# Seven-product gate projection in two more token groups, q weighted by another engine, stores on another queue

## The chip, the cores, the metric

One core of one Trainium2 chip. The metric is the device time of one execution in microseconds (us), median of several runs. Every run used below is in the fast state; a difference of half a per cent matters here, so most kernels were timed in five rounds beside the kernel before, on the same chip.

## The reference

q, k, v are 8 x 8 x 576 x 64 (batches, heads, positions, head size).

```python
r = np.maximum(x, 0.0); phi = np.concatenate([r * cos_w, r * sin_w], axis=-1)   # for q and k
kv  = np.einsum('bhsf,bhsd->bhfd', k_p, v);  z = np.sum(k_p, axis=2)
x   = np.einsum('bhsf,bhfd->bhsd', q_p, kv) / (np.einsum('bhsf,bhf->bhs', q_p, z) + 1e-06)
g   = x @ w_gate                     # x as 4608 tokens x 512, w_gate and w_val 512 x 1536
out = (silu(g) * (x @ w_val)) @ w_out
```

## The kernel before

It works through nine groups of 512 tokens (0 to 8). A group has a **gate and value stage** (gate = x W_gate, silu, times x W_val) and an **output stage** (times W_out). Beside these, TensorE makes the x tiles of the next group (four of 128 tokens each) and, once per batch, the product kv. The other work of attention is laid into numbered slots: a group has 16, twelve in the gate and value stage and four in the output.

TensorE's products land in banks of PSUM, and in this program a product waits until the bank that it writes has been read. In the groups of `GATE` the gate is made block-wise with seven products in place of eight (sums and differences of blocks first, then fewer products). Everything on an engine runs in the order in which it was issued, and that order is what the change works on:

```python
GATE = (7, 8)
...
for u in range(3):                       # ffn_by_quarters: a third of the gate each
    product(a, u, A11, B11, True)
    nc.scalar.copy(out=b, in_=a)         # PSUM to PSUM
    product(e, u, W3, X3, True)          # W: differences of weights, X: differences of x
    nc.scalar.copy(out=m7, in_=e)
    V(...)                               # one row of the value projection
    done()                               # the slot: an x tile, kv, a step of q, k or v
    product(b, u, W2, X2, False)
    nc.vector.tensor_tensor(out=c, in0=m7, in1=b, op=ALU.add)      # "the c add"
    product(a, u, A12, B21, False)
    silu(u, 1, 0, a)                     # ScalarE
    if u:
        mul(u - 1, 1, 1)                 # VectorE: silu times value, gives ht
    V(...); done()
    product(b, u, W1, X1, False)
    nc.vector.tensor_tensor(out=m7, in0=m7, in1=b, op=ALU.add)
    ...                                  # two more products, silus, values, muls
    if u == 2:
        for n in (1, 2):
            token_sum(n, 0, 4)           # VectorE: sums of ht for the output's seven products
    mul(u, 0, 0)
    mul(u, 1, 0)
    ...
def load_behind(b):                      # loads of batch b, once the turn of batch b-1 has landed
    nc.gpsimd.tensor_copy(out=hold2, in_=phit[b - 1][0:1, :, 0, 0, 0])
    load(b, "q")
    if b > 3:
        load_kv(b)
```

An x tile is a TensorE product and three VectorE operations (sum, reciprocal, multiply: 1.06 us), then a transposing DMA (its "turn"). A q batch is relu on ScalarE, a cosine and sine weighting on VectorE (0.75 us for each of four head pairs), then two transposing DMAs. kv leaves PSUM by two copies on ScalarE and, after them, two on VectorE.

Of the kernel before, what the change touches and what calls it, by code (L numbers as in the profile page):

```python
# [18 lines left out]
def kernel(  # L19
# [10 lines left out]
    nc = tc.nc  # L30
# [20 lines left out]
    KH = KC // 2  # L51
    GATE = (7, 8)

# [223 lines left out]
    def phi_q(b, g):  # L277

        if g == 0:
# [4 lines left out]
                                in1=tab, op=ALU.mult)  # L284

    def vmul(b, g):
        nc.vector.tensor_tensor(  # L287
            out=v2s[b == 1][:, g, :, :, 0:D],
            in0=(first if b == 0 and g == 0 else {"v": raw_of(b, "v")})["v"][:, g].unsqueeze(2).to_broadcast([P, NC, 2, D]),
            in1=tab, op=ALU.mult,  # L290
        )
# [144 lines left out]

    def a_tile2(t):

        (b0, c0), (b1, c1) = (divmod(2 * t + r, NC) for r in range(2))
        ps = take(2)  # L440
        if b0 == b1:
            parts = [(slice(0, P), b0, c0, 2)]
        else:
            parts = [(slice(0, SH), b0, c0, 1), (slice(SH, P), b1, c1, 1)]
        for e in range(2):
            for g in range(G):
                for ms, b, c, n in parts:
                    nc.tensor.matmul(  # L448
                        out=ps[ms, e, g * D1:(g + 1) * D1],
                        lhsT=phit[b][:, e, g, c:c + n].rearrange("p c s -> p (c s)"),  # L450
                        rhs=kv2s[b % 2][:, e, g // 2, g % 2], start=True, stop=True,
                    )
        x_of(t, ps)

# [152 lines left out]
    def ffn_by_quarters(tg, slot_of):  # L607
# [37 lines left out]
        for u in range(3):  # L645
# [12 lines left out]
            c = bank("c", seeded=True)  # L658
            nc.vector.tensor_tensor(out=c, in0=m7, in1=b, op=ALU.add)
            product(a, u, A12, B21, False)  # L660
            silu(u, 1, 0, a)
            free("a")
            if u:
                mul(u - 1, 1, 1)
            V(u, 0, 0) if u else V(u, 1, 0)
            done()
            product(b, u, W1, X1, False)
            nc.vector.tensor_tensor(out=m7, in0=m7, in1=b, op=ALU.add)
            silu(u, 0, 1, m7)
            product(c, u, A22, X4, False)  # L670
            silu(u, 0, 0, c)
# [16 lines left out]
            if u:  # L688
                done()
                token_sum(*((3, 0, 4) if u == 1 else (4, 0, 4)))  # L690
        V(2, 1, 1)
# [29 lines left out]

    def ffn_out(t, f0=0, f1=None):

        f1 = FC if f1 is None else f1
        if f0 == 0:
            o_ps[t] = take(1, ("o", t), fills=True)
        r = t % OUT * P
        for fc in range(f0, f1):
            nc.tensor.matmul(out=o_ps[t], lhsT=ht[:, fc, r:r + P], rhs=wo_sb[:, fc],  # L729
                             start=(fc == 0), stop=(fc == FC - 1))  # L730
        if f1 < FC:
            return
        ps = o_ps.pop(t)
        give_back(("o", t))
        if t % 2 == 0:
            nc.scalar.mul(out=ob_of(t), in_=ps, mul=DOWN)
        else:
            nc.vector.tensor_single_scalar(out=ob_of(t), in_=ps, scalar=DOWN, op=ALU.mult)
        store(t)

# [26 lines left out]
    def out_by_quarters(tg, slot_of):  # L767

        last = tg == NTG - 1
        t0 = tg * OUT  # L770
        for t in (t0, t0 + 2):
# [43 lines left out]
        for p_, o_, x_ in each(b, c[0], C22):  # L815
            nc.vector.scalar_tensor_tensor(out=o_, in0=x_, scalar=UP, in1=p_, op0=ALU.mult, op1=ALU.add)
        token_sum(4, 4, 6)
        slot_of(0)
# [14 lines left out]
        if last:  # L833
            store_two(t0 + 2, slice(0, HD))
        else:
            for t in (t0 + 2, t0 + 3):
                store(t)
        slot_of(2)
# [3 lines left out]
        for t in (t0, t0 + 1):  # L842
            store(t, *((slice(HD, d_model), (nc.sync, nc.scalar)) if last else ()))
        slot_of(3)
# [151 lines left out]
    def load_behind(b):  # L996

        nc.gpsimd.tensor_copy(out=hold2, in_=phit[b - 1][0:1, :, 0, 0, 0])  # L998
        load(b, "q")
        if b > 3:  # L1000
            load_kv(b)

    def load_kv(b):
# [14 lines left out]
    for b in range(2, B):  # L1018
        s0 = SLOTS * (b - 1)
        keng = "dve" if b == 2 else "act"  # L1020
        steps = [lambda b=b, g=g: phi_q(b, g) for g in range(G)]
        steps += [lambda b=b, g=g: (relu_k(b, g, g + 1, keng), vmul(b, g)) for g in range(G)]
        if b == 2:
            fs, tq = [s0 + i for i in (0, 0, 1, 1, 4, 5, 5, 6)], (s0 + 2, s0 + 2)
        else:
# [4 lines left out]
            at(p0 + 3 if b < 5 else p0 + 1, lambda b=b: load_behind(b))  # L1030
        tk = (s0 + 4, s0 + {2: 8, 3: 7}.get(b, 5))
        for s, f in zip(fs, steps):
# [5 lines left out]
    for t in range(2 * OUT, NTG * OUT):  # L1038
        tg, i = divmod(t, OUT)
        s = SLOTS * (tg - 1) + (5 if tg > 2 else 4) + 2 * i  # L1040
        if t == 2 * OUT:
            at(s, a_(t, 0))
            at(s + 1, a_(t, 1), turn(t))
        elif tg == 2:
            at((9, 10, 11)[i - 1] + SLOTS, lambda t=t: a_tile2(t), turn(t))
            if i == 2:
                at(11 + SLOTS, load_3)
        else:
            if t in (13, 14, 15):
                s = SLOTS * 2 + t - 4  # L1050
            elif tg - 1 in GATE:
                s = SLOTS * (tg - 1) + ((1, 2, 7, 9) if tg < 6 else (1, 2, 4, 7) if tg < 8 else (1, 2, 5, 6))[i]
            at(s, lambda t=t: a_tile2(t), turn(t))
    for tg in range(1, NTG):
# [12 lines left out]
        for i in range(OUT):  # L1067
            ffn_out(tg * OUT + i)
            weight_sum(i)
# [32 lines left out]
```

## Time and profile before

| what | value |
|---|---|
| time | 316.44 us (316.44 to 316.55, 3 runs) |
| span of the profiled execution | 314.5 us, clock 1.00 |
| TensorE | 98% busy, 2696 matmuls |

The page gives busy time by engine, the stretches view the same between two times, and the timeline lists single operations: start, length, engine, source line, operation, output and input by name, and in brackets how long the engine sat idle before it and what released it. The prediction below shows the main lines. One more place is needed for the comparison, the output stage of group 4, from the timeline of the kernel before:

```profile
175.80 1.47 PE L786 MATMUL banks<-wo_sb,ht 128*128 128x256 f16 x12
177.10 2.78 PE L786 MATMUL banks<-wt_sb,sums 128*128 128x256 f16 x24
179.11 1.25 ACT L266 ACTIVATE raw_q<-raw_q 128x576 bf16<-128x576 bf16 x2
179.72 1.47 PE L786 MATMUL banks<-wo_sb,ht 128*128 128x256 f16 x12
```

TensorE runs its first 48 output products without a bracket, that is without waiting. Later in this stage it pauses for 0.21 us before the last twelve products and for 0.12 us after them, by the starts of its rows against its pace. ScalarE's relus of the next q stand behind the silus of the group, in the output stage.

### The profile page before, as it was taken

The numbers are of one execution on the slowest core, as the hardware profiler recorded it, in microseconds if no ns is written. First come the engines' busy times: TensorE is split into PE (matmuls) and PEld (weight loads), VectorE is DVE, ScalarE is ACT, GpSimd is POOL, SyncE is SP. The second block draws the span as 40 slices with busy tenths as digits, with TensorE's granted clock in tenths as the row PEclk, the third lists the DMA queues.
The fourth block names the chain that finished last, engine by engine and source line by source line (L and its number), as shares of the span: only waits on it lengthen the run. The fifth ranks groups of instructions, "written<-read, shape, count | busy, mean of one in ns | idle before, by whom it ended". The sixth has DMA issues, their size and how long they took to land.

```text
span 314.5 us, 6775 instructions
## 1 busy us (share of the span) xinstructions
PE 307.5 (98%) x2696; PEld 189.7 (60%) x2696; DVE 228.2 (73%) x458; ACT 143.4 (46%) x264; POOL 36.0 (11%) x62
## 2 busy tenths in 40 slices
PE   8899999999999999999999999999999999999994
PEld 4597455455444585548654764577456866687673
DVE  7873777697678888587748786778779478946772
ACT  7554545763335346334543454335533345324530
POOL 7855102000200200030003000300000000000000
PEclk9999999999999999999999999999999999999999
DMA  7999999996897994989495979598951160014004
GB/s 268 217 198 197 206 205 138 226 133 99 143 208 114 150 145 110 148 119 196 100 153 75 200 144 154 73 192 135 164 86 35 40 145 17 20 38 98 0 2 133
DMA packets 74767, 41.07 MB, mean 131 GB/s; under 512 B 49904, under 2 KB 69872, under 8 KB 74736
## 3 DMA queue, kind: packets, MB, share of 16 engines
q1 hardware_dynamic: 51952, 22.55, 38.0%
q0 software_dynamic: 22192, 17.57, 37.2%
q10 hardware_dynamic: 592, 0.52, 0.5%
q8 instruction: 21, 0.34, 0.4%
q14 instruction: 10, 0.08, 0.1%
HBM read 37.75 MB, written 9.44 MB: 150 GB/s over the span
## 4 chain that ended last, share of the span: by engine, by line
PE 91%; DVE 5%; ACT 2%; issue 1%; ACTq 0%
PE banks L564 46%; PE banks L786 20%; PE banks L729 6%; PE banks L633 5%; PE banks L621 5%; PE banks L333 3%; PE banks L448 3%; DVE ht L638 1%; PE banks L494 1%; PE banks L430 1%; DVE v L287 1%; DVE sums L760 1%; DVE x L471 1%; PE banks L197 1%; PE banks L536 0%
## 5 line engine op out<-in xcount | busy, mean ns | idle before, releaser
L564 PE MATMUL banks<-xT,wg_sb 128*128 128x512 f16 (+2 forms) x368 | 86.6, 360 | 0.0
L564 PE MATMUL banks<-xT,wv_sb 128*128 128x512 f16 (+2 forms) x368 | 86.6, 360 | 0.0
L570 ACT ACTIVATE sg<-banks 128x512 bf16<-128x512 f32 (+2 forms) x92 | 51.5, 560 | 76.0 <-PE banks L564 74.0
L575 DVE TENSOR_TENSOR ht<-sg,banks 128x512 f16<-128x512 bf16 (+2 forms) x92 | 57.9, 637 | 29.7 <-PE banks L564 22.7
L564 PEld LDWEIGHTS <-wv_sb 128*128 128x128 f16 x368 | 35.5, 98 | 37.4
L564 PEld LDWEIGHTS <-wg_sb 128*128 128x128 f16 x368 | 33.9, 98 | 31.5 <-issue 0.2
L786 PEld LDWEIGHTS <-ht 128*128 128x128 f16 x336 | 32.5, 98 | 4.2
L786 PEld LDWEIGHTS <-sums 128*128 128x128 f16 x252 | 24.5, 98 | 4.2 <-issue 0.8
L633 PE MATMUL banks<-xT,wv_sb 128*128 128x512 f16 x96 | 24.3, 379 | 0.0
L283 DVE TENSOR_TENSOR r_q<-raw_q,tab 128x1152 bf16<-128x1152 bf16 x24 | 17.6, 754 | 7.4 <-ACT raw_q L266 7.1
L729 PE MATMUL banks<-wo_sb,ht 128*128 128x512 f16 x96 | 22.7, 379 | 0.0
L471 DVE TENSOR_TENSOR x<-banks,rec 128x512 f16<-128x512 f32 (+1 forms) x32 | 21.6, 674 | 1.3 <-PE banks L430 0.3
L786 PE MATMUL banks<-wo_sb,ht 128*128 128x256 f16 x168 | 20.6, 273 | 0.0
L287 DVE TENSOR_TENSOR v<-raw_v,tab 128x1152 bf16<-128x1152 bf16 x27 | 19.9, 751 | 0.5 <-ACT raw_v L849 0.5
L786 PE MATMUL banks<-wt_sb,sums 128*128 128x256 f16 x168 | 19.8, 273 | 0.1
L786 PE MATMUL banks<-wt_sb,ht 128*128 128x256 f16 x168 | 19.5, 273 | 0.0
L799 ACT ACTIVATE ob<-banks 128x512 f32<-128x512 f32 x14 | 8.4, 597 | 21.9 <-PE banks L786 21.9
L638 DVE TENSOR_TENSOR ht<-sg,banks 128x512 f16<-128x512 bf16 x24 | 15.5, 681 | 2.4 <-ACT sg L627 2.4
L266 ACT ACTIVATE raw_k<-raw_k 128x576 bf16<-128x576 bf16 (+1 forms) x25 | 17.1, 694 | 0.0
L998 POOL COPY hold<-phit 1x2 bf16<-1x2 bf16 x5 | 1.4, 287 | 129.3 <-DMA phit<-r_q 129.3
L760 DVE TENSOR_TENSOR sums<-ht 128x1024 f16<-128x1024 f16 (+1 forms) x28 | 15.5, 553 | 0.4
L266 ACT ACTIVATE raw_q<-raw_q 128x576 bf16<-128x576 bf16 x24 | 15.4, 675 | 0.0
(121 smaller groups left out, 334.6 us busy)
## 6 DMA issues: line engine op xcount, KB each, us to landing
out_dram<-ob SPq DMA_DIRECT2D x67, 128.0 KB, 2.5
raw_k<-in_k_dram POOLq DMA_DIRECT2D x7, 576.0 KB, 8.8
raw_q<-in_q_dram POOLq DMA_DIRECT2D x6, 576.0 KB, 6.0
raw_v<-in_v_dram POOLq DMA_DIRECT2D x6, 576.0 KB, 11.4
wo_sb<-in_moe_w_out_dram POOLq DMA_DIRECT2D x3, 512.0 KB, 12.8
wg_sb<-in_moe_w_gate_dram POOLq DMA_DIRECT2D x5, 256.0 KB, 9.4
wv_sb<-in_moe_w_val_dram POOLq DMA_DIRECT2D x5, 256.0 KB, 9.5
wo_sb<-in_v_dram SPq DMA_DIRECT2D x2, 576.0 KB, 4.0
```

The lines of the kernel that those rows point to most:

```text
L266: nc.scalar.activation(out=out, in_=in_, func=AF.Relu)
L283: nc.vector.tensor_tensor(out=st[b, "q"][:, g], in0=o.unsqueeze(2).to_broadcast([P, NC, 2, D]), in1=tab, op=ALU.mult)
L287: nc.vector.tensor_tensor(out=v2s[b == 1][:, g, :, :, 0:D], in0=(first if b == 0 and g == 0 else {"v": raw_of(b, "v")})["v"][:, g].unsquee ...
L471: nc.vector.tensor_tensor(out=st["x", t].rearrange("p (y e d) -> p e y d", e=2, d=D)[:, :, ys], in0=ps[:, :, 0:2 * J * D1].rearrange("p e ...
L564: nc.tensor.matmul(out=st["f", tg, fc, lo][i], lhsT=(wg_sb, wv_sb)[i][:, kc, fs], rhs=xT[tg][:, ts, kc], start=(kc == 0), stop=(kc == KC - 1))
L570: nc.scalar.activation(out=sg[:, 0:n], in_=st["f", tg, fc, lo][0], func=AF.Silu, scale=DOWN)
L575: nc.vector.tensor_tensor(out=ht[:, fc, r:r + n], in0=st.pop(("s", tg, fc, lo))[:, 0:n], in1=ps[1], op=ALU.mult)
L633: nc.tensor.matmul(out=val[u, i, w], lhsT=wv_sb[:, kc, fc * P:(fc + 1) * P], rhs=xT[tg][:, :, kc], start=(kc == 0), stop=(kc == KC - 1))
L638: nc.vector.tensor_tensor(out=ht[:, fc], in0=gates[u, w][:, i], in1=val.pop((u, i, w)), op=ALU.mult)
L729: nc.tensor.matmul(out=o_ps[t], lhsT=ht[:, fc, r:r + P], rhs=wo_sb[:, fc], start=(fc == 0), stop=(fc == FC - 1))
L760: nc.vector.tensor_tensor(out=o[:, lo:hi], in0=x[:, lo:hi], in1=y[:, lo:hi], op=op)
L786: nc.tensor.matmul(out=to[i][:, 0] if len(to) == 2 else to[0][:, i], lhsT=a[:, kc, i * P:(i + 1) * P], rhs=b[:, kc], start=first and kc == ...
```

## The change

The intent: save TensorE time in each of groups 5 and 6 (the prediction works out 1.21 us), and take work and waits out of VectorE's way there, so that the saving arrives.

```diff
-    GATE = (7, 8)
+    PHI_ACT = 7
+    GATE = (5, 6, 7, 8)
+    def phi_q_part(b, c, w):                       # q of batch 7: relu(cos * q) in one ScalarE pass
+        nc.scalar.activation(out=st[b, "q"][:, :, c, w], in_=raws[b, "q"][:, :, c], func=AF.Relu,
+                             scale=csk[:, c, w:w + 1])
 ... a_tile2 (an x tile)
-        x_of(t, ps)
+        if later:
+            behind.append(lambda: (x_of(t, ps), give_back(("a2", t)), x_turn(t)))
+        else:
+            x_of(t, ps)
 ... ffn_by_quarters
             nc.vector.tensor_tensor(out=c, in0=m7, in1=b, op=ALU.add)
+            while behind:
+                behind.pop(0)()
-            if u:
-                mul(u - 1, 1, 1)
 ...
             silu(u, 0, 1, m7)
+            if u:
+                mul(u - 1, 1, 1)
 ...
-                token_sum(*((3, 0, 4) if u == 1 else (4, 0, 4)))
+            if u == 1:
+                token_sum(3, 0, 4)
 ... out_by_quarters, groups 1 to 7
+        queues = (nc.gpsimd, nc.gpsimd) if tg > 0 else None
-        token_sum(4, 4, 6)
+        token_sum(4, 0 if tg in GATE else 4, 6)
-                store(t)
+                store(t, queues=queues)
 ... load_behind: q of batch 7 is loaded with batch 6
+        if PHI_ACT <= b + 1 < B:
+            load(b + 1, "q")
 ... slots of q, k, v (p0: first slot of the group before), kv, and x tiles
+            if b >= PHI_ACT:
+                for i in range(2 * NC):
+                    at(p0 + 4 + i // 2, lambda b=b, i=i: phi_q_part(b, *divmod(i, 2)))
+                fs, tq = [p0 + 12, p0 + 13, p0 + 14, p0 + 15], (p0 + 13, p0 + 13)
+            elif b > 3:
+                f0 = p0 + {4: 12, 5: 10}.get(b, 8)
+                fs, tq = [f0 + i for i in (...)], ...
-        tk = (s0 + 4, s0 + {2: 8, 3: 7}.get(b, 5))
+        tk = (s0 + 4, s0 + (3 if b - 1 in GATE else {2: 8, 3: 7}.get(b, 5)))
-                s = SLOTS * (tg - 1) + ((1, 2, 7, 9) if tg < 6 else (1, 2, 4, 7) if tg < 8 else (1, 2, 5, 6))[i]
+                s = SLOTS * (tg - 1) + ((0, 3, 7, 9) if tg < 6 else (0, 2, 5, 7) if tg < 8 else (0, 3, 5, 7))[i]
+                if s % SLOTS in (0, 3, 7):
+                    at(s, lambda t=t: a_tile2(t, True))
+                    continue
+            elif tg in GATE:                       # x tiles made in group 4: slots 5, 7, 9, 11 before
+                s = SLOTS * (tg - 1) + (2, 4, 7, 9)[i]
 ... (some small lines left out)
```

More of the change, by code (lines that the diff above doesn't have):

```diff
@@ L284, in phi_q @@
                                 in1=tab, op=ALU.mult)
+    def phi_q_part(b, c, w):
+        if (b, "q") not in st:
+            st[b, "q"] = rel.tile([P, G, NC, 2, D], BF16, name="r_q")
+        nc.scalar.activation(out=st[b, "q"][:, :, c, w], in_=raws[b, "q"][:, :, c], func=AF.Relu,
+                             scale=csk[:, c, w:w + 1])
     def vmul(b, g):
@@ L435, in a_tile, with a_tile2 @@
                 )
-    def a_tile2(t):
+    behind = []
+    def a_tile2(t, later=False):
         (b0, c0), (b1, c1) = (divmod(2 * t + r, NC) for r in range(2))
-        ps = take(2)
+        ps = take(2, ("a2", t) if later else None)
         if b0 == b1:
@@ L720, in store_two, with ffn_out @@
                 in_=obs[t // 2][e * SH:(e + 1) * SH, :, cols])
-    def ffn_out(t, f0=0, f1=None):
+    def ffn_out(t, f0=0, f1=None, queues=None):
         f1 = FC if f1 is None else f1
@@ L836, in out_by_quarters @@
             for t in (t0 + 2, t0 + 3):
-                store(t)
+                store(t, queues=queues)
         slot_of(2)
@@ L842, in out_by_quarters @@
         for t in (t0, t0 + 1):
-            store(t, *((slice(HD, d_model), (nc.sync, nc.scalar)) if last else ()))
+            store(t, *((slice(HD, d_model), (nc.sync, nc.scalar)) if last else (slice(0, d_model), queues)))
         slot_of(3)
@@ L998, in load_behind @@
         nc.gpsimd.tensor_copy(out=hold2, in_=phit[b - 1][0:1, :, 0, 0, 0])
-        load(b, "q")
+        if b < PHI_ACT:
+            load(b, "q")
         if b > 3:
             load_kv(b)
+        if PHI_ACT <= b + 1 < B:
+            load(b + 1, "q")
     def load_kv(b):
@@ L1020 @@
         keng = "dve" if b == 2 else "act"
-        steps = [lambda b=b, g=g: phi_q(b, g) for g in range(G)]
+        steps = [lambda b=b, g=g: phi_q(b, g) for g in range(G)] if b < PHI_ACT else []
         steps += [lambda b=b, g=g: (relu_k(b, g, g + 1, keng), vmul(b, g)) for g in range(G)]
@@ L1030 @@
             at(p0 + 3 if b < 5 else p0 + 1, lambda b=b: load_behind(b))
-        tk = (s0 + 4, s0 + {2: 8, 3: 7}.get(b, 5))
+            if b >= PHI_ACT:
[4 more added lines that the diff above has]
+                f0 = p0 + {4: 12, 5: 10}.get(b, 8)
+                fs, tq = [f0 + i for i in ((0, 0, 1, 2, 3, 4, 5, 6) if b == 4 else range(8))], (f0 + (3 if b == 4 else 4),) * 2
+        tk = (s0 + 4, s0 + (3 if b - 1 in GATE else {2: 8, 3: 7}.get(b, 5)))
         for s, f in zip(fs, steps):
@@ L1067 @@
         for i in range(OUT):
-            ffn_out(tg * OUT + i)
+            ffn_out(tg * OUT + i, queues=(nc.gpsimd, nc.gpsimd))
             weight_sum(i)
```

## The prediction

> **What bounds the kernel now.** I read the page of the profile first: its list of engines and the chain that ended last.
>
> ```profile
> PE 307.5 (98%) x2696; PEld 189.7 (60%) x2696; DVE 228.2 (73%) x458; ACT 143.4 (46%) x264; POOL 36.0 (11%) x62
> ```
>
> TensorE is busy all through, and the chain is 91% TensorE. So a change pays by what it takes off TensorE's stream of matmuls, and costs by every gap it puts into it. Next I cut the trace at the starts of the token groups (512 tokens each), by the stretches view; columns are the stretch, its length, then PE, PEld, DVE, ACT, POOL busy, clock, DMA share, GB/s. The rows are groups 4, 5, 6, 7; 7 (and 8) already form the gate projection from seven block products.
>
> ```profile
> 152.70:185.32 32.62, 32.59 (x294) 19.46 (x292) 24.14 (x46) 14.85 (x27) 2.40 (x4) 1.00 0.83 140
> 185.32:217.83 32.51, 32.48 (x285) 19.70 (x286) 24.74 (x47) 14.85 (x27) 2.91 (x4) 1.00 0.87 141
> 217.83:250.26 32.43, 32.43 (x295) 19.69 (x293) 23.13 (x45) 12.27 (x22) 0.00 (x0) 1.00 0.49 86
> 250.26:281.13 30.87, 30.37 (x251) 22.07 (x249) 22.95 (x45) 12.26 (x22) 0.00 (x0) 1.00 0.24 52
> ```
>
> Group 7 has 1.6 us less than group 6, but 1.18 of that is a kv product it has not got. The chain in order of time (start, length, what) gives TensorE's pace: 16 matmuls of 512 columns in 3.45 us, 215.6 ns each; 8 of 256 in 0.87, 108.8 ns each.
>
> ```profile
> 130.67 1.18 PE banks L333 x71
> 132.21 3.45 PE banks L564 x16
> 250.26 0.87 PE banks L621 x8
> 251.13 0.86 PE banks L633 x4
> ```
>
> At this pace group 7 needs 84 x 0.1088 (gate) + 48 x 0.2156 (value) + 4 x 0.26 (attention tiles) + 9.33 (output, as in other groups) = 29.9 us. It took 30.87: 1.0 us of gaps. TensorE's and then VectorE's rows of the timeline show two of them (start, length, ..., idle before).
>
> ```profile
> 256.26 0.60 PE L621 MATMUL banks<-xT,wg_sb 128*128 128x256 f16 x4
> 257.20 0.60 PE L621 MATMUL banks<-kvt,wgs_sb 128*128 128x256 f16 x4 [0.35 <-DVE x L471]
> ```
>
> ```profile
> 274.36 0.43 DVE L760 TENSOR_TENSOR sums<-ht 128x512 f16<-128x512 f16 x1
> ```
>
> The matmuls of 256.26 were issued by 256.70; the next waited until 257.20, 0.5 us, for the bank that the x step was reading. The token sum of 274.36 ends at 274.79, and the output product that reads it goes on at 274.84, 0.6 us late. A seven-product group lives at VectorE's limit.
>
> **What the Trainium skill says.** "TensorE: Matmul & The Clock Gate", section "Back-to-back issue gap", gives N/2.4 + 2.5 ns: 216 for 512 columns, 109 for 256. The trace agrees (215.6, 108.8); the page's "sustained" 131 ns for 512 it does not show. "PSUM — Partial Sum Buffer", section "PSUM bank collisions raise a hardware error", wants accesses of ScalarE and VectorE to one bank guarded; so VectorE's kv copies wait for ScalarE's, in the list of waits 6.6 us over 6. "Trainium Kernel Development and Optimization", section "Key Constraints", says that issuing from another engine saves issue time alone, as all queues share the DMA engines. In the trace a GpSimd issue occupies it 0.75 us. "ScalarE: Activation LUTs", section "What it computes", has func(scale * in + bias): relu and cosine weight in one pass.
>
> **The change part by part.** *Seven products in groups 5 and 6.* Out: 48 x 0.2156 = 10.35 us. In: 84 x 0.1088 = 9.14. Saved 1.21 us a group on the path, 2.4 in all: 0.8% of 316.4. This is the ceiling of the intent. It adds per group: 6 adds of 0.6 us on VectorE (start to start in a row), 4 input sums of 0.43, and 6 ScalarE copies of 0.58.
>
> *The last q by ScalarE.* 8 operations less on VectorE and ScalarE (4 x 0.754, 4 x 0.675), 18 of 256 columns in. ScalarE's relu takes 675 ns for 576 columns and 1156 for 1152, so 0.19 + 0.00084 per column: 0.41 us each, an estimate, 7.3 us in group 5. ScalarE has room (about 12 busy before), but in order: two of these in front of a silu delay its multiply by up to 0.8.
>
> *Stores on GpSimd's queue.* 56 issues x 0.75 = some 42 us of an engine at 11%. The transposes on the sync queue no longer queue behind eight stores (about 5.8 us). TensorE waits for no transpose now, so this itself gives nothing; it allows the earlier slots.
>
> *Group 4.* The order of instructions shows q's weighting moved from the output slots into slots 8 to 11, three of the four (0.72 each) ahead of the last token sum. Before, that sum ended 1.5 us after the output stage began (177.42 against 175.96), with VectorE almost without idle from 168.8. It will end at about 1.5 + 2.2 = 3.7; the product reading it needs it 2 x 1.31 + 0.44 = 3.06 after the start. **Loss 0.6.**
>
> *Group 5, by walking its order with these durations.* Its first product with a difference of x waits for the weight sum (0.95): 0.1. After slot 2 the same bank as in group 7 waits for x: 0.5. Then the kv product: after it ScalarE copies (0.76), VectorE copies (0.87), then c's add (0.69), with latencies 2.5 us, as the three muls leave no more work ahead; TensorE has only two products and a value row, 0.44 + 0.44 + 0.86 = 1.74. Loss 0.75, in group 5 the value row's bank even waits for the silu: 0.85. At the output some 0.15. Total 1.6 against 1.21 saved: **+0.4**. *Group 6:* the same without the weight sum, 1.3: **+0.1**.
>
> *Group 7.* The first x is put behind c's add, the second goes to slot 3, and one token sum (0.6) moves into the output stage. Left is about 0.45 for a bank at slot 3 and 0.1 at the output, of 1.0: **-0.4**. Groups 0 to 3 and 8: nothing.
>
> Sum: 0.6 + 0.4 + 0.1 - 0.4 = +0.7, so 317.1 from the walk. The gaps overlap less well on paper than on a chip (where one engine is late, the next wait shrinks), and the change is plainly laid out to avoid them; without any gap it would be 316.44 - 2.4 - 0.9 = 313.1. I choose 316.2, some three quarters of the way from 313.1 to 317.1.
>
> **Rivals.** (1) *The gaps are filled.* For it: deferred x steps, a mul moved behind an add, and group 8, already of this kind, whose gate and value stage ran without gaps. Against: groups 5 and 6 also have kv, x and, in 5, v's weighting. It would make 313 to 314.5. (2) *VectorE becomes the bound.* In group 5 it has some 22.7 us of work before the output against TensorE's 21.7; if it idles where it waits for kv, the stage becomes 24 and the time 317.5 to 318. (3) *GpSimd gets late.* Loads stand behind eight stores in its order (6 us), and the next q, k, v come later: in groups 3 to 5 ScalarE would wait for them. Against: loads are issued a third of a group ahead of use, and take 6 to 11 us. A miss would cost 1 to 3 us. (4) *ScalarE's 18 small passes* delay silus: up to 0.8 more in group 5.
>
> **Range and chances.** The walk and the gapless case differ by 4 us; I take 314.4 to 317.8, most of it. 2% is 6.3 us: a gain of that size exceeds the ceiling, and a loss needs two rivals at once. Faster 0.02, within 0.96, slower 0.02. Which side of 316.44 is nearly a coin toss, with a little more on faster.
>
> **What would show it.** Per-group stretches: groups 5 and 6 at 32.0 to 32.9 say the walk holds, 31.2 to 31.5 that the gaps are filled; group 7 at 30.2 to 30.5; group 4 longer by about 0.6. TensorE's matmuls should be 2696 - 192 + 264 = 2768. In the timeline I expect a TensorE gap of 0.7 to 0.9 just after kv in groups 5 and 6, and one before the last token sum of group 4. ScalarE's new passes should take about 0.4 us. Wrong would be: waits of ScalarE for DMA of q or k, a lower granted clock, or q passes far over 0.4.

## The result, and the profile after

The changed kernel took **318.56 us** (318.43 to 318.69, 4 runs), the kernel before beside it 316.5 (316.44 to 316.94). The ratio is 1.006 [1.0045, 1.008]: same by the 2% rule, but 2.1 us slower, and outside the predicted range. A ratio is the mean time of one kernel's fast runs over that of the other's in the same rounds, so it isn't quite the ratio of the medians.

From the page of the changed kernel, the engines; then, from its stretches view, groups 4, 5, 6 and 7 (stretch, length, then PE, PEld, DVE, ACT, POOL busy, clock, DMA share, GB/s):

```profile
PE 305.5 (96%) x2768; PEld 196.1 (62%) x2768; DVE 235.7 (74%) x470; ACT 154.0 (49%) x290; POOL 65.8 (21%) x118
```

```profile
152.84:186.32 33.48, 32.77 (x294) 19.47 (x292) 26.84 (x50) 15.77 (x29) 7.24 (x14) 1.00 1.10 169
186.32:219.11 32.79, 31.74 (x323) 23.04 (x320) 27.05 (x51) 22.33 (x48) 5.95 (x12) 1.00 0.68 121
219.11:251.96 32.85, 31.83 (x330) 23.03 (x328) 24.39 (x47) 13.80 (x26) 4.21 (x9) 1.00 0.35 68
251.96:282.42 30.46, 30.20 (x250) 22.04 (x248) 22.82 (x44) 12.25 (x22) 4.17 (x9) 1.00 0.22 53
```

TensorE is busy 2.0 us less (2.4 were intended), in a span of 316.6 us that is 2.1 longer. Groups 5 and 6 have only 31.7 to 31.8 us of TensorE work in 32.8 us: one microsecond of gaps in each, where the rows of the kernel before had almost none. Group 4, whose products didn't change, is 0.74 us longer than the 32.74 that the trace of before gives with the same cut (the rows in the prediction are cut up to 0.2 us later).

The trace, cut at the first matmul of each stage, gives the whole sum. Lengths in us, gate and value stage + output stage:

| group | before | after | difference |
|---|---|---|---|
| up to group 3 | 120.14 | 120.45 | +0.31 |
| 3 | 23.04 + 9.36 | 23.03 + 9.36 | 0 |
| 4 | 23.26 + 9.48 | 23.26 + **10.22** | +0.74 |
| 5 | 23.03 + 9.36 | 23.37 + 9.42 | +0.40 |
| 6 | 23.25 + 9.18 | 23.43 + 9.42 | +0.42 |
| 7 | 21.45 + 9.42 | 20.96 + 9.50 | -0.41 |
| 8 | 19.53 + 9.47 | 19.53 + 9.59 | +0.12 |
| from TensorE's end to the last record | 4.52 | 5.10 | +0.58 |

That is 2.16, and the spans differ by 2.1. Only 1.15 of it lies in groups 4 to 7; the start, the tail and group 8 are taken up further below. Where do group 4's 0.74 come from? Its timeline, after:

```profile
172.05 0.68 ACT L267 ACTIVATE raw_q<-raw_q 128x576 bf16<-128x576 bf16 x1 [1.39 <-DMA raw_q<-in_q_dram]
...
176.35 0.68 DVE L587 TENSOR_TENSOR ht<-sg,banks 128x512 f16<-128x512 bf16 x1
...
177.08 0.94 PE L802 MATMUL banks<-wo_sb,ht 128*128 128x256 f16 x7 [0.27 <-DVE ht L587]
...
180.20 1.05 PE L802 MATMUL banks<-wt_sb,sums 128*128 128x256 f16 x8 [0.44 <-DVE sums L775]
```

Two places. At 180.20 is the last token sum, the gap that the prediction worked out (0.60 us against TensorE's pace). At 172.05 is the other one: ScalarE stood still for 1.39 us until the load of q had landed, since its relu was moved ahead of the last silus. The silus, VectorE's weighting and multiplies come late in turn, and at 177.08 TensorE waits for ht, 0.43 us. The two gaps make 1.03 us and the stage is 0.74 us longer, because the two pauses that the kernel before has later in this stage are gone. (A gap is the time from the end of the matmul before, at TensorE's pace, to the next start; the bracket shows less, as it counts from the modelled end.)

The load was issued earlier too, but not as much earlier as the relu. GpSimd's issue of it, before and then after:

```profile
170.10 0.74 POOL L131 DMA_DIRECT2D raw_q<-in_q_dram  x1 [0.28 <-PE banks L564]
```

```profile
165.96 0.79 POOL L132 DMA_DIRECT2D raw_q<-in_q_dram  x1 [0.32 <-issue]
```

The issue moved up by 4.1 us, the first relu from 179.11 to 172.05, by 7.1 us, and it would have started 1.39 us sooner still.

In group 6, timeline after:

```profile
226.22 0.60 PE L633 MATMUL banks<-kvt,wgs_sb 128*128 128x256 f16 x4 [0.35 <-DVE x L483]
...
229.70 0.87 DVE L363 CAST kv<-banks 64x260 bf16<-64x260 f32 x2 [1.75 <-ACT kv L363]
...
230.60 0.70 DVE L671 TENSOR_TENSOR banks<-m,banks 128x512 f32<-128x512 f32 x1
...
231.35 0.60 PE L633 MATMUL banks<-kvt,wgs_sb 128*128 128x256 f16 x4 [0.65 <-DVE banks L671]
```

The first wait is the bank that the x step of slot 2 reads (gap 0.51 us). The second is the c add (L671), which stands on VectorE behind the kv copies, and these behind ScalarE's (gap 0.82). Group 5 has the same two, 0.51 and 0.85. These were predicted at 0.5 and 0.75 to 0.85.

The 18 new ScalarE passes take 498 ns each, one every 0.40 us or so (two in 0.89); 0.41 was estimated. The stores, from the pages' lists of DMA issues (count, KB, median us to landing), before and after:

```profile
out_dram<-ob SPq DMA_DIRECT2D x67, 128.0 KB, 2.5
```

```profile
out_dram<-ob POOLq DMA_DIRECT2D x56, 128.0 KB, 5.4
```

From GpSimd's queue a store takes about twice as long to land. Whether that matters is for the experiments.

### The profile page after: what moved, and what is told of

Its sections match the earlier page's. It is cut to its first block, busy times and chain, and to the rows that moved or that the text cites. A ratio compares the mean times of both kernels' runs of the same rounds, so it can differ in the third digit from the quotient of the medians.

```text
span 316.6 us, 6938 instructions
## 1 busy us (share of the span) xinstructions
PE 305.5 (96%) x2768; PEld 196.1 (62%) x2768; DVE 235.7 (74%) x470; ACT 154.0 (49%) x290; POOL 65.8 (21%) x118
## 5 line engine op out<-in xcount | busy, mean ns | idle before, releaser
L576 PE MATMUL banks<-xT,wg_sb 128*128 128x512 f16 (+2 forms) x272 | 62.0, 354 | 0.0
L576 PE MATMUL banks<-xT,wv_sb 128*128 128x512 f16 (+2 forms) x272 | 62.0, 354 | 0.0
L582 ACT ACTIVATE sg<-banks 128x512 bf16<-128x512 f32 (+2 forms) x68 | 37.1, 547 | 50.2 <-PE banks L576 49.6
L587 DVE TENSOR_TENSOR ht<-sg,banks 128x512 f16<-128x512 bf16 (+2 forms) x68 | 41.6, 621 | 22.4 <-PE banks L576 15.6
L726 POOL DMA_DIRECT2D out_dram<-ob x56 | 29.4, 534 | 130.7 <-ACT ob L815 126.0
L645 PE MATMUL banks<-xT,wv_sb 128*128 128x512 f16 x192 | 48.6, 379 | 0.7 <-ACT sg L639 0.7
L650 DVE TENSOR_TENSOR ht<-sg,banks 128x512 f16<-128x512 bf16 x48 | 30.7, 680 | 3.0 <-ACT sg L639 3.0
L639 ACT ACTIVATE sg<-banks 128x512 bf16<-128x512 f32 x36 | 20.6, 590 | 12.6 <-PE banks L633 12.5
L633 PEld LDWEIGHTS <-wgs_sb 128*128 128x128 f16 x192 | 17.8, 98 | 8.8 <-issue 2.0
L633 PE MATMUL banks<-kvt,wgs_sb 128*128 128x256 f16 x144 | 21.6, 273 | 1.3 <-DVE x L483 0.7
```

The costliest lines, as they stand in the source:

```text
L576: nc.tensor.matmul(out=st["f", tg, fc, lo][i], lhsT=(wg_sb, wv_sb)[i][:, kc, fs], rhs=xT[tg][:, ts, kc], start=(kc == 0), stop=(kc == KC - 1))
L582: nc.scalar.activation(out=sg[:, 0:n], in_=st["f", tg, fc, lo][0], func=AF.Silu, scale=DOWN)
L587: nc.vector.tensor_tensor(out=ht[:, fc, r:r + n], in0=st.pop(("s", tg, fc, lo))[:, 0:n], in1=ps[1], op=ALU.mult)
L633: nc.tensor.matmul(out=to[:, i], lhsT=a[:, c, 2 * u + i], rhs=x[:, :, c], start=first and i == 0 and c == 0, stop=c == KH - 1, skip_group_ ...
L639: nc.scalar.activation(out=gates[u, w][:, :, j * HT:(j + 1) * HT], in_=src, func=AF.Silu, scale=DOWN)
L645: nc.tensor.matmul(out=val[u, i, w], lhsT=wv_sb[:, kc, fc * P:(fc + 1) * P], rhs=xT[tg][:, :, kc], start=(kc == 0), stop=(kc == KC - 1))
```

## The experiments

Eighteen kernels ran, each in five rounds beside the kernel before, all with the right result but one, which was wrong on purpose. The lengths that they rest on, in us (stage + output):

| kernel | time | group 3 | group 4 | group 5 | group 6 | group 7 |
|---|---|---|---|---|---|---|
| before | 316.5 | 32.40 | 23.26 + 9.48 | 23.03 + 9.36 | 23.25 + 9.18 | 30.87 |
| after | 318.56 | 32.39 | 23.26 + 10.22 | 23.37 + 9.42 | 23.43 + 9.42 | 30.46 |
| e9_after_again | 319.48 | 32.39 | 23.26 + 11.60 | 23.36 + 9.42 | 23.43 + 9.42 | 30.44 |
| e1_stores_sync | 319.84 | 32.39 | 23.26 + 11.16 | 23.36 + 9.42 | 23.44 + 9.42 | 30.38 |
| e2_before_stores_gpsimd | 316.35 | 32.39 | 23.27 + 9.36 | 23.03 + 9.36 | 23.25 + 9.18 | 30.76 |
| e3_q6_scalar | 317.11 | 32.96 | 23.27 + 9.17 | 23.36 + 9.43 | 23.43 + 9.43 | 30.38 |
| e6_gate_7_8 | 318.43 | 32.39 | 23.26 + 9.93 | 24.98 + 9.17 | 23.26 + 9.17 | 29.98 |
| e12_q6_slots_of_before | 319.41 | 32.39 | 23.26 + 9.36 | 25.38 + 9.42 | 23.43 + 9.43 | 30.43 |
| e5_kv_slot_2 | 319.87 | 32.39 | 23.27 + 11.09 | 23.82 + 9.42 | 23.72 + 9.43 | 30.51 |
| e10_kv_copies_behind | 318.26 | 32.39 | 23.26 + 10.34 | 22.07 + 10.44 | 22.91 + 10.34 | 29.98 |
| e11_q6_scalar_kv_behind | 316.89 | 33.71 | 23.27 + 9.17 | 22.07 + 10.68 | 22.91 + 10.33 | 29.99 |
| e13_sums_left_out | 315.61 | 32.40 | 23.25 + 11.00 | 22.06 + 9.17 | 22.91 + 9.17 | 29.99 |
| e17_kv_on_scalar | 317.38 | 32.87 | 23.28 + 9.17 | 22.06 + 10.44 | 23.50 + 10.33 | 29.99 |
| e19_order_only | 314.29 | 32.59 | 23.51 + 9.17 | 22.67 + 9.41 | 22.62 + 9.17 | 29.74 |

### Which part loses: stores, q, or the seven products

**Stores back on the sync queue**, all else as changed.

```diff
-        queues = (nc.gpsimd, nc.gpsimd) if tg > 0 else None
+        queues = None
```

> The changed kernel with its 56 stores back on the sync queue. Theory (the 2.1 us are gaps of TensorE in groups 4 to 6 plus 0.6 at the end and 0.3 at the start): the groups stay (group 4 output stage 10.2 us, groups 5 and 6 32.8 us each); if GpSimd's stores make the end longer, the tail from TensorE's end to the last instruction falls from 5.1 to 4.5 us and the time to about 318.0; if the 0.9 us at start and end are scatter from run to run, the time stays at 318.3 to 318.7. Rival (stores on GpSimd's queue are what lets q be weighted earlier): phit comes later, a wait for it appears in groups 4 or 5 and the time is 319 or more.

319.84 us (319.71 to 319.98), ratio 1.010 [1.008, 1.011]. In its trace group 4's output is 11.16 us, with ScalarE 2.33 us idle for the q load; groups 5 to 7 are as in the changed kernel. The time is one that the rival expected (319 or more), but the wait is for the load of raw q, not for phit, and the changed kernel itself has it. So GpSimd's queue isn't where the time went.

**The kernel before, with its stores on GpSimd's queue.**

> The kernel before with only its stores moved to GpSimd's queue. If the queue costs time at the end: 316.5 + 0.6 = about 317.1, with the tail at 5.1 us. If scatter: 316.5 within 0.2. The groups' lengths stay as before (32.4 to 32.6) in both.

316.35 us, ratio 0.998 [0.997, 0.9996], no stage longer and the tail 4.5 us. Its stores take 4.3 us to land (median) in place of 2.5, and that costs nothing here.

**Batch 6's q by ScalarE too**, so that neither relu nor weighting of it stands in group 4.

```diff
-    PHI_ACT = 7
+    PHI_ACT = 6
```

> The changed kernel with q of batch 6 too weighted by ScalarE, so that VectorE has four operations of 0.75 us less in group 4. Theory (these stand ahead of the token sum): group 4's output stage falls from 10.22 to 9.4 us and the time by 0.7, to about 317.8. Rival (ScalarE's 18 passes delay silus in group 4, or q comes late by DMA): stage of group 4 grows over 23.3, no gain.

317.11 us, ratio 1.001 [0.9998, 1.002]. Both gaps of group 4's output are gone (9.17 us), where 9.4 and a time of 317.8 us had been expected. A new one stands one group earlier, at the first product of group 4, from its timeline:

```profile
153.16 1.04 PE L576 MATMUL banks<-xT,wg_sb 128*128 128x512 f16 x4 [0.41 <-DMA xT<-x]
```

This setting also loads the extra q one group earlier, and the last turn of x now lands late (gap 0.57 us). In the stretch from 132 to 156 us the GpSimd queue carried 2.36 MB in place of 1.77, and the x turns landed in 9.5 us, not 7.5.

**Seven products in groups 7 and 8 only**, the rest of the change kept.

```diff
-    GATE = (5, 6, 7, 8)
+    GATE = (7, 8)
```

> The changed kernel with seven products in groups 7 and 8 only, as before; all other parts stay. Theory: groups 5 and 6 at 32.4 to 32.6 each as before, group 7 at 30.4, so 318.5 - 0.8 = about 317.7, still above the kernel before by group 4's gap, if that is still there, and the tail; if q's weighting ahead of the token sum costs in group 5 too, more. Rival (the seven products do gain 2.4 and something else loses): the time goes up to about 320.

318.43 us (317.08 to 319.0), ratio 1.0045 [1.003, 1.006]. That is over the 317.7 expected. Group 6 is back at 32.43, but group 5 is 34.15 us. Its timeline:

```profile
198.91 0.91 ACT L290 ACTIVATE r_q<-raw_q,cs_all 128x256 bf16<-128x256 bf16 x2 [4.45 <-DMA phit<-r_q]
...
199.72 0.58 ACT L582 ACTIVATE sg<-banks 128x512 bf16<-128x512 f32 x1
...
200.35 1.02 PE L576 MATMUL banks<-xT,wg_sb 128*128 128x512 f16 x4 [0.72 <-ACT sg L582]
```

The first of ScalarE's q passes waited for the turn of the q before it to leave the buffer, and the silu stood behind it. This kernel doesn't isolate the seven products, as I had meant it to; it shows the pattern of group 4 a second time: an operation that waits for a transfer, ahead of a silu on ScalarE's queue.

**The changed kernel once more**, unaltered.

> The changed kernel unaltered, run again to see what of its 2.1 us repeats. Theory 'the gaps are the cause': the lengths of the stages and outputs of groups 3 to 8 repeat to 0.1 us (their sum is 1.2 to 1.3 us over the kernel before), and the rest (0.31 us before group 3, 0.58 us in the tail) is scatter of the transfers and moves by some tenths: time 317.8 to 318.7, ratio 1.003 to 1.006. Rival 'the tail belongs to the change': the tail from TensorE's last product to the last instruction is again 5.1 us and not 4.5, and the ratio is 1.006 or more.

319.48 us, and its runs spread from 317.77 to 319.92. All stages from group 3 on repeat to 0.05 us but one, group 4's output: 11.60 us. From its timeline:

```profile
173.59 0.68 ACT L267 ACTIVATE raw_q<-raw_q 128x576 bf16<-128x576 bf16 x1 [2.77 <-DMA raw_q<-in_q_dram]
...
178.62 0.94 PE L802 MATMUL banks<-wo_sb,ht 128*128 128x256 f16 x7 [1.64 <-DVE ht L587]
```

ScalarE's wait is 2.77 in place of 1.39 us, and TensorE's gap 1.81 in place of 0.43: one to one. The load was issued at 166.75 in place of 165.96, and from issue to relu it took 6.8 us in place of 6.1. So this wait is a matter of when the load lands. It is the only stage that differs between the two traces, and so the likely source of the changed kernel's scatter. The time is over the theory's 317.8 to 318.7, and both marks of the rival (ratio, tail) are there, though it is group 4 that raised the ratio. The tail of 5.1 us came again. Over all traces it is either about 4.5 or 5.1 (once 5.45) us: 4.5 in all nine with `PHI_ACT` 6, 5.1 or more in six of nine with 7, the changed kernel's two among them. What decides it isn't settled.

**Batch 6's q back in the slots of before**, all else as changed.

```diff
-            elif b > 3:
+            elif b > 3 and b != 6:
```

> The changed kernel with the weighting and turn of batch 6's q put back to the slots that the kernel before uses (four and more slots later), all else as changed. Theory 'in group 4's slots 8 to 11 ScalarE's relu of q waits for the q load to land, and holds up silu, multiply and token sum': ScalarE has no wait for raw q ahead of a silu there, group 4's output is 9.4 to 9.6 us (10.2 and 11.6 us in two runs of the changed kernel), time 0.7 to 2 us under the changed kernel, and its runs scatter by less than 0.5 us where those of the changed kernel spread over 2 us. Rival 'VectorE is simply full there': group 4's output stays over 10 us, or the next stage grows by as much.

Half hit, half miss. Group 4's output is 9.36 us, so the moved slots were its cause. But the time is 319.41 us: group 5's stage grew to 25.38, and there VectorE comes late to the differences of x and to the c add, behind v's multiplies, which moved along. The scatter, expected under 0.5 us, was 1.1 (318.8 to 319.93). The changed kernel's early slots do buy something; they are paid for in group 4.

### The gaps of groups 5 and 6

**kv one slot earlier, an x tile put off.**

```diff
-        tk = (s0 + 4, s0 + (3 if b - 1 in GATE else {2: 8, 3: 7}.get(b, 5)))
+        tk = (s0 + 4, s0 + (2 if b - 1 in GATE else {2: 8, 3: 7}.get(b, 5)))
-                s = ... ((0, 3, 7, 9) if tg < 6 else (0, 2, 5, 7) if tg < 8 else (0, 3, 5, 7))[i]
+                s = ... ((0, 3, 7, 9) if tg < 6 else (0, 3, 5, 7))[i]
```

> The changed kernel with the kv product and its two PSUM copies one slot earlier in groups 5 to 7 (slot 2 for slot 3) and the second x tile of groups 5 and 6 at slot 3, so put off behind the c add. Theory 'copies and x steps ahead of the c add cost 0.5 and 0.85 us in each of groups 5 and 6': the stages of groups 5 and 6 fall from 23.37 and 23.43 us by 0.5 to 1.3 us each, time 0.8 to 2.2 us under the changed kernel run beside it. Rival 'TensorE waits anyway, whatever stands in these slots': both stages stay within 0.2 us and gaps of the same size stand at other products.

A miss: 319.87 us, stages of 23.82 and 23.72. The two gaps of 0.51 and 0.8 became one of 1.65, where TensorE waits for the bank that three multiplies behind VectorE's kv copies free.

**The same with batch 6's q on ScalarE, and then with the extra q load moved later.**

> e5_kv_slot_2 with batch 6's q weighted by ScalarE too (PHI_ACT 6). If the two repairs add up (group 4's output 9.2 us in place of 10.2, groups 5 and 6 as in e5_kv_slot_2, group 3's output 9.9 us with its gap of 0.57 us), the time is 1.0 us under e5_kv_slot_2 and 0.4 to 1.2 us under the kernel before. If VectorE and ScalarE only pass the work to each other, it is no faster than e5_kv_slot_2.

318.35 us: group 4 is repaired as in e3_q6_scalar, groups 5 and 6 are as bad as in e5_kv_slot_2, and the time isn't 0.4 to 1.2 us under the kernel before, as had been expected. The two act independently.

```diff
-        if PHI_ACT <= b + 1 < B:          # in load_behind
-            load(b + 1, "q")
+            if PHI_ACT <= b + 1 < B:
+                at(p0 + 14, lambda b=b: load(b + 1, "q"))
```

> e7_q6_scalar_kv_slot_2 with the extra load of q moved from the second slot of its group to the output stage. Theory 'the gap of 0.57 us at the end of group 3's output is the extra 576 KB load holding up the turn of x on the DMA engines': the gap goes, group 3's output is 9.4 us again, time 0.4 to 0.6 us under e7_q6_scalar_kv_slot_2. Rival 'the gap comes of ScalarE or VectorE, which have the same work there': group 3's output stays at 9.9 us. A third way: the late load holds up the turn of q, and a new gap stands in group 4's stage.

325.97 us, the third way of the expectation: group 3's output is 9.35 us again, so the load was what held up the turn of x. But the turn of q took its place: it had landed by 170.98 us (the copy on GpSimd that waits for it starts then), in the changed kernel by 165.47. Group 4's stage is 31.58 us. ScalarE stands idle for 9.52 us until 171.23, when its first pass on the next q may start; its bracket names the turn of x, but the turn of q, for which the same pass waits in e6_gate_7_8, had landed just then, and is the likelier cause. The silu behind it is what TensorE's bracket names: gaps of 4.23, 1.15 and 0.36 us at an x tile. And then the next twelve products of 512 columns took 4.99 us where 2.59 is their pace; the granted clock was 0.77 between 165 and 180 us. That is 2.4 us more, which came with the wait.

**kv's copies put behind the c add**, the second x tile at slot 5. (The expectation says groups 4 to 7; the edit works where both kv and seven products are, in groups 5 and 6.)

```diff
-        at(tk[-1], lambda b=b: kv_mm(b), lambda b=b: kv_out2(b))
+        at(tk[-1], lambda b=b: kv_mm(b), (lambda b=b: behind.append(lambda: kv_out2(b)))
+           if b - 1 in GATE else (lambda b=b: kv_out2(b)))
-                s = ... ((0, 3, 7, 9) if tg < 6 else (0, 2, 5, 7) if tg < 8 else (0, 3, 5, 7))[i]
+                s = ... ((0, 5, 7, 9) if tg < 8 else (0, 3, 5, 7))[i]
```

> The changed kernel with the two copies of kv out of PSUM put behind the c add in groups 4 to 7 (as the x steps of some slots are), and the second x tile of groups 5 and 6 at slot 5 in place of 2. Theory 'the order on VectorE and ScalarE ahead of the c add makes both gaps': the gap of 0.51 us at slot 2 and that of 0.82 to 0.85 us after the kv product go, the stages of groups 5 and 6 fall from 23.37 and 23.43 us to 22.1 to 22.6 each, 1.6 to 2.4 us in all. Rival 'a group with kv and x has no slack on VectorE, so a gap put off comes back': new gaps at slots 4 to 7, stages no more than 0.5 us shorter each. Group 4's output stays 10.2 to 11.6 us.

Both theories were half right. Group 5's stage fell by 1.30 us to 22.07, which is TensorE's own work but for 0.15 us at an x tile. Group 6's fell by only 0.52: its gap at slot 2 went, but 0.84 us after the kv product stayed, where TensorE waits for a silu. And group 5's output grew by 1.02. Timeline of group 5's end:

```profile
206.99 0.69 DVE L483 TENSOR_TENSOR x<-banks,rec 128x512 f16<-128x512 f32 x1
207.60 0.68 DVE L775 TENSOR_TENSOR ht<-ht 128x1024 f16<-128x1024 f16 x1
...
208.32 0.69 DVE L775 TENSOR_TENSOR sums<-ht 128x1024 f16<-128x1024 f16 x1
...
208.93 1.28 DVE L650 TENSOR_TENSOR ht<-sg,banks 128x512 f16<-128x512 bf16 x2
...
209.66 0.28 PE L802 MATMUL banks<-wo_sb,ht 128*128 128x256 f16 x1 [0.55 <-DVE ht L650]
```

VectorE does an x step (slot 9), two token sums and only then the multiplies that the output's first products read. Time 318.26 us.

**The same with batch 6's q on ScalarE.**

> e10_kv_copies_behind with batch 6's q weighted by ScalarE too. If group 4's output is repaired as in e3_q6_scalar (9.17 us) and group 3's output costs 0.3 to 0.6 us for the load, the time is 0.5 to 1.5 us under e10_kv_copies_behind; with the stages of groups 5 and 6 at 22.1 to 22.6 us it is 315.0 to 316.2 us, under the kernel before.

316.89 us, level with the kernel before (ratio 1.0004) and over the 315.0 to 316.2 expected. Group 3's output cost 1.3 us this time. That gap scatters too: over the eight traces with the extra load early in group 3, its output takes 9.5 to 10.8 us.

**Amount or order? Two token sums left out** in groups 5 and 6 (wrong on purpose: the output reads old sums).

```diff
-            if u == 2:
+            if u == 2 and tg not in (5, 6):
                 for n in (1, 2):
                     token_sum(n, 0, 4)
```

> e10_kv_copies_behind with two token sums of 128x1024 left out of the last third of the gate and value stage in groups 5 and 6 (the output then reads the sums of the group before: wrong on purpose). It takes 2 x 0.6 us from VectorE just ahead of the output. Theory 'VectorE's amount of work before the output sets the time there': the gaps of 0.71 and 0.48 us at the start of group 5's output and of 0.61 and 0.48 us in group 6's shrink together by 1.0 us each to about 0.2, both outputs are 9.4 to 9.5 us (10.44 and 10.34), time 1.6 to 2.0 us under e10_kv_copies_behind (318.26). Rival 'the multiplies come late because of the silus and latencies, not of work': the outputs stay over 10.1 us.

Confirmed: outputs of 9.17 us in both, no gap at all, and 315.61 us though group 4's output happened to be 11.00. So 1.2 us of VectorE just ahead of the output is what the multiplies wait behind.

**The sums on GpSimd** (correct result), with the x tiles of group 3 one slot earlier.

```diff
                 for n in (1, 2):
-                    token_sum(n, 0, 4)
+                    token_sum(n, 0, 4, nc.gpsimd)
```

> e15_x_of_g4_early with the same two token sums done by GpSimd in groups 5 to 8 (right result). If GpSimd does one in under 1.5 us and VectorE isn't slowed, outputs of groups 5 and 6 are 9.4 to 9.6 us and the time is 1.5 to 2 us under e15_x_of_g4_early, 314.5 to 315.2. If GpSimd is slow (over 2.5 us each), the product that reads the sums waits, outputs are over 11 us and the time is over 318.

A miss, 318.2 us, level with e15_x_of_g4_early below (318.17), the outputs 10.82 and 10.60. Its timeline:

```profile
206.17 2.12 POOL L775 TENSOR_TENSOR ht<-ht 128x1024 f16<-128x1024 f16 x1 [9.83 <-DVE ht L650]
...
208.37 2.12 POOL L775 TENSOR_TENSOR sums<-ht 128x1024 f16<-128x1024 f16 x1
...
208.65 2.12 DVE L775 TENSOR_TENSOR sums<-ht 128x512 f16<-128x512 f16 x1
```

GpSimd takes 2.12 us for what VectorE does in 0.69, and the VectorE sum beside it took 2.12 us too, in place of 0.42. The Trainium skill, "SBUF — State Buffer", section "Who interferes with whom", says that a VectorE instruction with two SBUF inputs contends with a GpSimd instruction that reads SBUF, and that the ports they share are an exclusive lock; the trace agrees. (Beside GpSimd's first sum, VectorE's multiplies with one input in PSUM took their usual time, two in 1.27 us.)

**x tiles of group 3 one slot earlier**, on top of e11_q6_scalar_kv_behind and of e3_q6_scalar.

```diff
-        s = SLOTS * (tg - 1) + (5 if tg > 2 else 4) + 2 * i
+        s = SLOTS * (tg - 1) + (5 if tg > 2 and tg != 4 else 4) + 2 * i
```

> e11_q6_scalar_kv_behind with the four x tiles made in group 3 one slot (about 1.6 us) earlier. Theory 'the first product of group 4 waits for the last turn of x, which the extra q load holds up': group 3's output falls from 10.67 us to 9.4 to 9.6, time 0.4 to 1.2 us under e11_q6_scalar_kv_behind (316.89). Rival 'the DMA engines are full until then whenever the turn starts': output stays at 9.9 us or more.

> e3_q6_scalar with the same earlier x tiles in group 3. By the same theory group 3's output falls from 9.92 to 9.4 us and the time from 317.1 to 316.5, level with the kernel before; groups 5 and 6 keep their stages of 23.4 us and their gaps.

318.17 us (317.18 to 319.55) and 317.41 us. Group 3's output was 9.50 us in one trace and 10.83 in the other. Inconclusive for the first, against the theory in the second: TensorE still waits for x's turn (1.16 us in its bracket) although that started at 145.05, 2.3 us earlier than in e3_q6_scalar. Starting earlier doesn't cure it.

**VectorE's kv copies to ScalarE.**

```diff
-        for w, eng in enumerate((nc.scalar.copy, nc.vector.tensor_copy)):
+        for w, eng in enumerate((nc.scalar.copy, nc.scalar.copy if b - 1 in GATE else nc.vector.tensor_copy)):
```

> e11_q6_scalar_kv_behind with all four kv copies on ScalarE in groups 4 to 7, none on VectorE. Theory 'VectorE's amount of work before the output sets the time': 0.87 us less on it, so the gaps at the start of the outputs of groups 5 and 6 (1.19 and 1.09 us together) fall to 0.2 to 0.5, outputs 9.5 to 9.8 us, time 1.2 to 1.7 us under e11_q6_scalar_kv_behind: 315.2 to 315.8 us, if group 3's output costs the same. Rival 'ScalarE's longer copies hold up the silus and so the multiplies': the stages of groups 5 and 6 grow by 0.4 to 0.8 us and the outputs stay over 10 us.

> e10_kv_copies_behind with the same move of the kv copies. The same fall of the outputs of groups 5 and 6 to 9.5 to 9.8 us, and group 4's output still 10.3 to 11.6 us; time 1.2 to 1.7 us under e10_kv_copies_behind (318.26): 316.6 to 317.1 us.

Misses, 317.38 and 318.89 us. VectorE has 0.87 us less to do in the stage, and the output of group 5 is 10.44 and 10.53 us: nothing gained. Group 6's stage grew from 22.91 to 23.50 in both, and the timeline of e17_kv_on_scalar shows why:

```profile
227.17 1.53 ACT L363 CAST kv<-banks 64x260 bf16<-64x260 f32 x4 [1.33 <-PE banks L340]
...
228.72 0.60 ACT L639 ACTIVATE sg<-banks 128x512 bf16<-128x512 f32 x1
...
229.37 0.81 PE L645 MATMUL banks<-xT,wv_sb 128*128 128x512 f16 x3 [1.27 <-ACT sg L639]
```

Together with e13_sums_left_out this tells apart what my theory had run together. 1.2 us less just ahead of the output helps, 0.87 us less in the middle doesn't: in e17_kv_on_scalar VectorE waits 0.97 us for TensorE where its kv copies had stood, and comes to the last x step with the same 0.27 us of idle time as before. It isn't the amount over the group, it is the order at its end.

**Order only.** All operations and results as in e11_q6_scalar_kv_behind; the x steps leave the last third, and two multiplies go ahead of the second sum. I picked these slots among some forty by replaying the orders with the durations and waits measured in the traces, which is an estimate.

```diff
-                s = ... ((0, 5, 7, 9) if tg < 8 else (0, 3, 5, 7))[i]
+                s = ... {6: (0, 4, 5, 7), 7: (0, 4, 5, 7), 8: (0, 3, 5, 7)}[tg][i]
             if u == 2:
-                for n in (1, 2):
-                    token_sum(n, 0, 4)
+                token_sum(1, 0, 4)
             mul(u, 0, 0)
             mul(u, 1, 0)
+            if u == 2:
+                token_sum(2, 0, 4)
```

> e11_q6_scalar_kv_behind with the x tiles of groups 5 and 6 at slots 0, 4, 5, 7 (none in the last third of the stage) and the two multiplies of slot 9 ahead of the second token sum, in all seven-product groups. The same operations in another order. Theory 'VectorE's order in the last third of the stage sets it': replaying the two orders with the durations measured in the traces (an estimate), the stages of groups 5 and 6 are 22.5 to 23.0 us and their outputs 9.2 to 9.6, so 32.2 and 31.9 us in all in place of 32.75 and 33.24, and group 7 loses 0.2 more; time 314.4 to 315.6 us, under the kernel before. Rival 'the amount of VectorE's work over the whole group sets it, and a gap put off comes back': the sum of stage and output stays at 32.7 to 33.2 us in both groups and the time at 316.5 or more.

**314.29 us** (314.09 to 314.45), ratio 0.991 [0.990, 0.993], with the right result: under both kernels, and 0.1 us below the expected range; groups 5 and 6 came within 0.12 us of the replay. Its groups 4 to 7 in the stretches view, and the end of group 5 in the timeline:

```profile
153.00:185.68 32.68, 32.66 (x292) 19.75 (x293) 24.08 (x46) 20.00 (x43) 6.28 (x12) 1.00 0.97 154
185.68:217.76 32.08, 31.75 (x323) 23.30 (x320) 26.78 (x51) 22.28 (x48) 6.11 (x12) 1.00 0.72 125
217.76:249.55 31.79, 31.42 (x330) 23.25 (x328) 24.12 (x47) 13.32 (x25) 4.02 (x9) 1.00 0.36 70
249.55:279.29 29.74, 29.74 (x251) 22.08 (x249) 22.64 (x44) 12.23 (x22) 4.17 (x9) 1.00 0.22 54
```

```profile
206.40 0.69 DVE L776 TENSOR_TENSOR ht<-ht 128x1024 f16<-128x1024 f16 x1
...
207.01 1.28 DVE L650 TENSOR_TENSOR ht<-sg,banks 128x512 f16<-128x512 bf16 x2
...
208.35 1.47 PE L803 MATMUL banks<-wo_sb,ht 128*128 128x256 f16 x12
```

The multiplies come right behind the first sum, at 207.01, ahead of the output's start, and its twelve products run without a wait. Group 5 has 26.78 us of VectorE work, nearly the 27.05 of the changed kernel, and takes 0.71 us less. Group 7 has no gap left. Against the kernel before, the trace has group 5 at -0.31, group 6 at -0.64, group 7 at -1.13 us. So the largest part of the gain is in group 7, which had its seven products before; groups 5 and 6 bring 0.95 of the 2.4 us that their products save. Its runs spread over 0.4 us.

The kernel before in these rounds had 317.09 us as its median, with one slow run of 535.91 that the ratio leaves out. Against the 316.44 to 316.74 of the other rounds, on other chips, the gain is 2.2 to 2.5 us, 0.7%; in its own round it is 2.8.

## Why the prediction was wrong, point by point

- **Saved per group: 1.21 us.** Right in the counts and the pace: TensorE did 2768 matmuls, as counted. The busy time of the span, whose ends are modelled, fell by 2.0 us and not 2.4. In e13_sums_left_out group 5 is 1.16 us shorter than before.
- **Group 5: +0.4; group 7: -0.4.** Measured +0.40 and -0.41. The walk through VectorE's order found each gap: 0.16 (0.1 predicted), 0.51 (0.5), 0.85 (0.85) and, at the output, 0.26 (0.15) in group 5, 0.41 (0.45) in group 7. One reading was off: before, the token sum of 274.36 kept TensorE waiting 0.26 us, and not 0.6. The 24 products around it took 2.87 us for a pace of 2.61.
- **Group 6: +0.1.** Measured +0.42. The term that was mis-sized is the sum of its gaps, 1.3. Its own parts, 0.5, 0.75 and 0.15, make 1.4; measured are 0.51, 0.82, 0.26 at the output and 0.14 at an x tile that was left out, 1.7 in all.
- **Group 4: +0.6.** The token sum's gap was 0.60 us, as worked out, but the 0.31 us of pauses that this stage had before are gone, which the walk didn't count: net, this gap costs some 0.3 (an estimate). The step that failed is what I left out of it: moving q's work to slots 8 to 11 also moved ScalarE's relu ahead of silus, before its load had landed. That adds 0.43 us in one trace and 1.81 in the other, in a kernel whose runs spread over 2.2 us; e12_q6_slots_of_before and e3_q6_scalar each remove the wait. The prediction had ScalarE waiting for q's load as the mark of a failure, under the rival "GpSimd gets late", but argued it away with the loads being issued a third of a group ahead of use. After the move the relu could have started 4.7 us after the issue of its load, and the load took 6.1. The mark showed, the cause was another: e1_stores_sync takes the stores off GpSimd and has the wait all the same.
- **Groups 0 to 3 and 8: nothing.** Group 8's output is 0.12 us longer. The 0.31 us before group 3 is within the scatter: over the traces the start of group 3 lies between 120.14 and 120.64, the changed kernel and the kernel before with other queues among them. The tail's 0.58 isn't explained. So a good part of the 2.1 us stays open: groups 4 to 7 hold 1.15 of it.
- **"The gaps overlap less well on paper than on a chip"**, by which 317.1 of the walk became 316.2. This is the step that failed most plainly, and it was a choice, not a working. The gaps of 0.51, 0.85, 0.82 and 0.60 came at nearly the walk's sizes, in the changed kernel's two traces and in e3_q6_scalar; where an edit removed one, another came later in the same group (e10_kv_copies_behind), until the amount (e13_sums_left_out) or the order (e19_order_only) was changed. Left at 317.1, and with the 0.3 that group 6 took more than predicted, the prediction would have been 1.2 us low and not 2.4.
- **"VectorE becomes the bound"** (rival 2) named the right engine, but by its amount of work. e17_kv_on_scalar and e19_order_only show that the order at the end of the stage decides.
- **18 passes of 0.41 us.** Right (0.40).
- **56 issues x 0.75 us on GpSimd, 42 us.** Measured 29.4, 0.53 each: the 0.75 was that of loads of 576 KB. No gap above hangs on it.

## What to carry to other kernels

When an operation is moved earlier on an in-order engine, look up what it waits for, and above all whether that is a transfer: everything behind it on that engine, here the silus, inherits the wait and its scatter. Saving products on the busiest engine pays only if the engine that feeds it is done in time at the point of hand-over; count what stands in its queue in the last microseconds before that point, not its share of busy time. And a walk through the orders with measured durations can be trusted to some tenths of a microsecond; a discount on it needs a reason as good as the walk.

## What the Trainium skill lacked or had wrong

- "GPSIMD Engine Reference", section "4.1 Engine selection", has an elementwise operation of two inputs at about twice VectorE's time on GpSimd. Here it was three times: 2.12 us against 0.69 for a 128 x 1024 sum of 16-bit numbers. That section doesn't mention what the move did to VectorE's own sum, 2.12 us in place of 0.42.
- "TensorE: Matmul & The Clock Gate", section "Back-to-back issue gap", has a sustained 131 ns for a matmul of 512 columns and keeps 216 for an isolated one. In the streams of these traces it is 215.6 ns.
- "DMA: Bandwidth & Descriptors", where it would belong, has no landing time of a store by issuing queue among other traffic: 5.4 us median from GpSimd's queue after, 2.5 from the sync queue before, for the same 128 KB. Nor how long a transposing transfer takes when loads are queued beside it: the x turns went from 7.5 to 9.5 us when one load of 576 KB was added to three.
